# A fused attention and expert kernel: filler products in a tile of their own, the near mask on VectorE, a replanned opening, coarse pairs one inner tile later

## The chip, the cores and the metric

The kernel runs on one core of a Trainium2 chip. The time is the device time of one execution in microseconds (us); three runs of the kernel before gave 1113.57, 1114.93 and 1112.37, median 1113.57. The profile is of one further execution of 1113.12 us, whose span from the first to the last instruction is 1111.3 us; 1.8 us of it lie around the span. Times inside the profile count from the start of the span. Engines: PE is TensorE (PEld its weight loads), DVE is VectorE, ACT is ScalarE, POOL is GpSimd, SP is SyncE, which here only issues transfers.

## The reference

Attention on 8 batches, 8 heads, 576 positions of 64 numbers, the sum of two parts, and behind it a gated feed-forward network over the 8 x 576 = 4608 tokens of 512 numbers:

```python
q_d = q.reshape(B, H, Sd, 4, D).mean(axis=3)          # also k_d, v_d: 144 coarse positions
out_up = np.repeat(sm_attn(q_d, k_d, v_d), 4, axis=2) # every coarse row serves 4 positions
mask = np.abs(pos[:, None] - pos[None, :]) < 4        # band: 7 neighbours
out_local = np.matmul(softmax(where(mask, scale * q @ k.T, -1e9)), v)
x = (out_up + out_local) as (4608, 512)
xn = x / sqrt(mean(x * x) + 1e-6) * rms_g
g = xn @ w_gate                                       # 512 x 1536
out = (g * sigmoid(g) * (xn @ w_val)) @ w_out         # 1536 x 512
```

All is float32.

## The kernel before, in words

**Tiling.** The 4608 tokens are 36 units of 128 tokens; two units make a chunk, so there are 18 chunks of 256 tokens. The feed-forward network of a chunk (class `Forward`) runs over six inner tiles of two 128-wide slices of the 1536: per inner tile 48 products into `ps_h` (L1371: gate and value, each with the high part of the activations against high and low weights and the low part against high weights, so that three products stand for one in float32) and 12 products into `ps_o` (L1409). Before that each chunk needs its activations `xh` and `xl`, turned by eight transposes (L1021) after the mean of squares (L998) and a root by Newton steps (L717 to L719).

**Coarse attention** (class `Coarse`): 32 pairs of heads, four per batch; each is scores (L582), a softmax with its maximum on DVE (L591, L596) and its exponentials on ACT (L601), two transposes (L611), values (L626) and a scaling on DVE (L644), stored to a buffer from which the chunks load it back. **Band attention** (class `Attention`): products with the seven neighbours and sums on DVE (L905, L909, L958, L968) and ACT (L951). Chunk 0 is made otherwise (class `Early`): its band scores run on TensorE. A product of `one_sb` (2^33 times the identity) with `near_sb` (0 on the band, -1 off it) puts the mask into `ps_h` (L1154), the scores are added (L1156), then come the maximum (L1169), the exponentials (L1180), shares, transposes (L1215, L1226), values (L1242), the coarse part (L1249), the copy, squares, root, and the transposes L1287 to `xh` and `xl` (L1290, L1294). `near_sb` is made on POOL by `make_near` from shifted copies of the identity (L1495 to L1501), `one_sb` by `make_one` (L1482).

**Weights** come as raw 64-bit numbers and are decoded in 20 pieces: ACT scales (L315), POOL makes the last bits (L325), DVE joins (L332), ACT rounds the high part (L339), DVE subtracts for the low part (L344, L346).

**What sets the order.** Chunks 0 to 2, band attention up to chunk 3, the first twelve coarse pairs and all decoding are written out by a planner (class `Plan`). Each task has an engine, a cost, a due time, what it follows, and the buffers it takes; `lag` is the time that the plan gives a transfer until it has landed. `RANK`, a table of one number per task, replaces the due times; among the tasks that could start soon on an engine, the lowest number goes first. The order in which the planner takes tasks is the order on each engine's queue, and an engine works its queue strictly in that order. The plan also counts how long TensorE would sit idle before a product (`plan.idle`: from the later of the engine being free and the output's buffer being free), and `heat` (L487 to L500, products at L497) fills 95% of that with filler products of zeros, 256 or 512 columns wide, into the very tile that the next real product will write. Fillers serve nothing but to keep TensorE running; they are a fixed number in the built program, whatever the real times are. From chunk 3 on a loop at the end of the kernel emits the chunk's inner tiles with the next chunk's band attention and two coarse pairs between them, at positions `at` counted in inner tiles; a scheduler settles the rest.

Of the kernel before, what the change touches and what calls it, by code (L numbers as in the profile page):

```python
# [19 lines left out]
P = 128  # L20
# [51 lines left out]
    2040, 2137, 1910, 1295, 1259, 1019, 310, 1083, 1192, 1302, 1748, 1186, 2074, 728, 581, 1321, 2278, 1403,
    1366, 1300, 478, 1512, 1140, 1422, 2046, 1341, 1818, 1238, 667, 1951, 2712, 705, 499, 1901, 2018, 1979,
    2204, 1663, 2103, 1559, 1364, 2075, 916, 2006, 1578, 1699, 2278, 1694, 2367, 1296, 945, 2057, 2643, 1490,
    1510, 1335, 647, 1488, 1579, 1553, 2177, 1304, 2400, 1216, 928, 1667, 2795, 1528, 623, 865, 1035, 1063,
    1094, 1140, 1175, 1800, 2532, 2260, 2066, 2133, 2082, 1659, 1303, 1722, 1285, 1871, 902, 1492, 1229, 1879,
    2256, 2114, 2247, 2458, 2052, 2710, 2316, 2168, 1624, 1870, 1180, 1676, 1980, 1947, 1114, 1296, 1153, 1252,
    1358, 1558, 1420, 2740, 3465, 3179, 2589, 2603, 2821, 3045, 2860, 3141, 2745, 3064, 1135, 2258, 2194, 2453,
    3436, 2937, 2304, 3002, 2299, 3135, 2188, 2846, 1869, 2301, 2073, 1141, 1769, 577, 481, 1035, 729, 1100,
    751, 1131, 1136, 862, 885, 880, 924, 1042, 1067, 1104, 1123, 1252, 1261, 1252, 1268, 1359, 1372, 1266, 1360,  # L80
    1420, 570, 2150, 3901, 229, 1873, 1297, 1427, 1613, 1616, 1493, 1251, 535, 535, 1692, 1181, 1845, 362, 555,
    1526, 1542, 1495, 628, 574, 1558, 1613, 1547, 870, 550, 1724, 1603, 1541, 603, 601, 1502, 1658, 1498, 694,
    803, 1717, 1787, 1623, 730, 803, 1703, 1639, 1759, 603, 734, 1750, 1834, 2679, -522, 1819, 2241, -707, 1556,
    2495, 1719, 1870, 1310, 1386, 526, 1897, 1097, 1237, 467, 1554, 1284, 1521, 1570, 1801, 1383, 1964, 2071,
    1442, 1062, 1458, 1178, 1526, 1413, 1545, 1354, 1672, 1477, 1972, 1505, 2000, 1646, 2226, 1714, 2927, 1604,
    2590, 2691, 2108, 3005, 1733, 1849, 2263, 2127, 2536, 2400, 966, 767, 1687, 2629, 2385, 1032, 962, 1533,
    2769, 2588, 1296, 1000, 1689, 2766, 2444, 972, 1085, 1618, 2709, 2557, 1174, 928, 1756, 2879, 2740, 1197,
    1227, 1795, 2940, 2486, 1020, 1328, 2029, 2881, 2625, 1211, 901, 1799, 3211, 2699, 1944, 2860, 2599, 2325,
    2363, 1854, 2569, 2085, 2452, 3285, 2105, 1880, 2515, 3410, 2111, 189, 468, 382, 275, 215, 340, 149, 612,
    398, 344, 331, 413, 78, 139, 223, -16, 297, 299, 123, 654, 206, 284, 379, 448, 339, 199, 372, 323, 372, 495,  # L90
    274, 501, 349, 374, 476, 297, 205, 639, 350, 599, 622, 633, 614, 767, 500, 501, 474, 392, 520, 627, 410,
    484, 625, 622, 738, 480, 476, 633, 631, 518, 580, 808, 579, 541, 574, 753, 639, 859, 633, 684, 355, 683,
    626, 881, 824, 574, 665, 579, 804, 789, 796, 575, 724, 899, 984, 1209, 799, 1007, 975, 999, 1035, 1216, 611,
    1024, 1136, 957, 342, 679, 455, 477, 1239, 948, 809, 917, 668, 748, 982, 1319, 253, 641, 541, 427, 941,
    1155, 248, 580, 450, 396, 1134, 1143, 769, 692, 810, 848, 716, 821, 633, 703, 871, 950, 1009, 771, 614, 817,
# [1539 lines left out]
```

## Time and profile before

| what | value |
| --- | --- |
| median of three runs | 1113.57 us |
| profiled execution, its span | 1113.12 us, 1111.3 us |
| PE busy | 1077.7 us, 97% |
| DVE, ACT, POOL busy | 924.4 (83%), 603.9 (54%), 194.5 us (18%) |
| L1371 products | 5184 |
| L1409 products | 1296 |
| first L1371 of chunk 0, of chunk 1, of chunk 3 | 88.69, 153.82, 274.31 us |
| granted clock of PE, mean | 0.982 |

How to read it: a row of the timeline or of a group gives a start, a duration, the engine, the line, the operation and the operands as out<-in, with a count behind "x"; what stands in square brackets is the idle time before it and what ended it. In rows of windows the pairs are busy microseconds and instruction counts of each engine. A float32 product counts as two matrix instructions where its operands are not of the rounded kind. PE's durations overlap, since products are pipelined; the distance between starts is the better measure.

### The profile page before, as it was taken

What the parts mean: (1) busy time and instruction counts of PE and PEld (TensorE: products, weight loads), DVE (VectorE), ACT (ScalarE), POOL (GpSimd) and SP (SyncE); (2) the same over time, 40 slices, a digit from 0 to 9 for tenths busy, and PEclk for the clock granted to TensorE, in tenths of its full rate; (3) what the DMA queues carried; (4) which work ended last, traced back from release to release, by engine and by line L of the source; (5) the groups of instructions that cost most, each with busy time, mean ns of one, the idle gap of its engine ahead of it and who ended that gap; (6) DMA issues with size and microseconds to landing.
All of it is one profiled execution on the core that took longest, in us unless ns stands there. A gap on an engine that the chain in (4) does not pass through costs nothing.

```text
span 1111.3 us, 21801 instructions
## 1 busy us (share of the span) xinstructions
PE 1077.7 (97%) x8013; PEld 982.0 (88%) x8013; DVE 924.4 (83%) x1554; ACT 603.9 (54%) x2068; POOL 194.5 (18%) x236
## 2 busy tenths in 40 slices
PE   5899899998999999999999999999999999999997
PEld 4668889897998999999999999999999999999997
DVE  6989988779989898988889898979797988986321
ACT  3865847473747373737474747373737273746111
POOL 8756645231210101010101001100000000000000
PEclk9689989999999999999999999999999999999999
DMA  9787536442663526161525243533131322210000
GB/s 324 261 270 196 132 92 140 96 104 83 136 145 79 131 77 148 50 153 53 138 70 134 64 129 82 130 74 101 39 106 44 96 70 78 72 50 19 1 21 19
DMA packets 79281, 116.84 MB, mean 105 GB/s; under 512 B 32015, under 2 KB 39351, under 8 KB 79173
## 3 DMA queue, kind: packets, MB, share of 16 engines
q1 hardware_dynamic: 47380, 90.50, 26.3%
q0 software_dynamic: 12128, 20.27, 11.5%
q10 hardware_dynamic: 19664, 4.66, 1.9%
q8 instruction: 63, 1.03, 0.4%
q14 instruction: 46, 0.37, 0.1%
HBM read 103.58 MB, written 11.80 MB: 104 GB/s over the span
## 4 chain that ended last, share of the span: by engine, by line
PE 75%; DVE 1%; POOL 0%; issue 0%; ACT 0%; DMA 0%; SPq 0%; DVEq 0%
PE ps_h L1371 45%; PE ps_o L1409 23%; PE ps_a L626 2%; PE ps_a L582 2%; PE ps_a L1021 1%; PE ps_a L611 1%; DVE prod L905 0%; PE ps_a L497 0%; POOL newton L721 0%; DMA q_t<-in_q_band_dram 0%; PE ps_a L998 0%; DVE sc L909 0%; SPq L894 0%; DVE x_t L1008 0%; DVE x_t L968 0%
## 5 line engine op out<-in xcount | busy, mean ns | idle before, releaser
L1371 PE MATMUL ps_h<-xh,w 128*128 128x256 f32 x3456 | 631.2, 280 | 1.4 <-ACT xh L1025 0.7
L1371 PEld LDWEIGHTS ps_h<-xh,w 128*128 128x128 f32 x3456 | 537.3, 188 | 11.1 <-issue 2.3
L1371 PE MATMUL ps_h<-xl,w 128*128 128x256 f32 x1728 | 482.6, 280 | 0.0
L1409 PE MATMUL ps_o<-wo,hs 128*128 128x512 f32 x1296 | 331.8, 399 | 1.8 <-POOL hs L1395 1.0
L1371 PEld LDWEIGHTS ps_h<-xl,w 128*128 128x128 f32 x1728 | 325.3, 188 | 6.5 <-issue 1.9
L951 ACT ACTIVATE prod<-kv,sc 128x64 f32<-128x64 f32 x1088 | 279.8, 407 | 29.5 <-DVE sc L942 20.4
L1409 PEld LDWEIGHTS ps_o<-wo,hs 128*128 128x128 f32 x1296 | 234.6, 190 | 48.1 <-issue 1.7
L968 DVE TENSOR_REDUCE x_t<-prod 128x128 f32<-128x896 f32 x136 | 143.2, 1078 | 42.6 <-PE ps_a L1021 36.7
L1378 ACT ACTIVATE sil<-ps_h 128x512 f32<-128x512 f32 x108 | 64.5, 597 | 159.3 <-PE ps_h L1371 146.8
L905 DVE TENSOR_TENSOR prod<-q_t,kv 128x896 f32<-128x896 f32 x136 | 148.2, 1094 | 1.1 <-DMA q_t<-in_q_band_dram 0.6
L1392 ACT ACTIVATE hs<-sil 128x512 fp32r<-128x512 f32 x108 | 68.1, 630 | 146.9 <-DVE sil L1386 137.8
L909 DVE TENSOR_REDUCE sc<-prod 128x14 f32<-128x896 f32 x136 | 145.1, 1076 | 0.5
L1381 DVE SCALAR_TENSOR_TENSOR sil<-sil,ps_h 128x512 f32<-128x512 f32 x108 | 73.7, 682 | 46.3 <-ACT sil L1378 45.9
L958 DVE TENSOR_TENSOR prod<-sc,kv 128x384 f32<-128x384 f32 (+1 forms) x136 | 110.8, 860 | 0.2
L417 POOL DMA_DIRECT2D qk<-in_qk_sum_dram x42 | 39.3, 963 | 372.1 <-DMA qk<-in_qk_sum_dram 324.3
L1386 DVE SCALAR_TENSOR_TENSOR sil<-sil,ps_h 128x512 f32<-128x512 f32 x108 | 74.4, 689 | 31.6 <-PE ps_h L1371 31.5
L1395 DVE TENSOR_TENSOR hs<-sil,hs 128x512 fp32r<-128x512 f32 x96 | 68.3, 711 | 18.0 <-ACT hs L1392 17.9
L991 ACT ACTIVATE up_t<-x_t 128x128 f32<-128x128 f32 x136 | 41.9, 308 | 47.7 <-DVE x_t L981 29.9
L601 ACT ACTIVATE a_g<-ps_a,m_g 72x144 f32<-72x144 f32 x128 | 46.4, 369 | 22.8 <-DVE m_g L596 21.0
L417 POOL DMA_DIRECT2D vs<-in_v_sum_dram x42 | 38.4, 914 | 82.2 <-DMA vs<-in_v_sum_dram 48.5
L582 PE MATMUL ps_a<-qk 64*72 64x144 f32 x256 | 32.4, 317 | 13.7 <-DVE qk L473 11.9
L691 ACT COPY a_g<-ps_a 72x288 f32<-72x288 f32 x57 | 20.9, 400 | 44.3 <-PE ps_a L611 44.1
(136 smaller groups left out, 851.9 us busy)
## 6 DMA issues: line engine op xcount, KB each, us to landing
kv<-in_k_pad_dram SPq DMA_DIRECT2D x60, 320.0 KB
kv<-in_v_pad_dram SPq DMA_DIRECT2D x60, 320.0 KB
qk<-in_qk_sum_dram POOLq DMA_DIRECT2D x42, 288.0 KB, 4.7
out_dram<-o_sb SPq DMA_DIRECT2D x96, 72.0 KB
vs<-in_v_sum_dram POOLq DMA_DIRECT2D x42, 144.0 KB, 4.1
q_t<-in_q_band_dram SPq DMA_DIRECT2D x150, 36.0 KB
w<-in_w_gate_dram SPq DMA_DIRECT2D x8, 512.0 KB
w<-in_w_val_dram SPq DMA_DIRECT2D x8, 512.0 KB
```

The source lines that it names most:

```text
L417: nc.gpsimd.dma_start(out=t, in_=(qk_sum, v_sum)[i][self.b, j, :, self.half], accum_op=ALU.add)
L905: nc.vector.tensor_tensor(out=pr, in0=bcast(q[:, s0:s0 + 2], 2, NO), in1=window(k, s0), op=ALU.mult)
L909: nc.vector.tensor_reduce(out=self.sc[:, j, par, s0:s0 + 2], in_=self.pr[i], axis=AX.X, op=ALU.add,)
L951: nc.scalar.activation(out=self.pr[i][:, o, s], in_=self.v[j, par][:, s0 + s + o], func=AF.Copy, scale=p[:, s, o:o + 1],)
L958: (nc.vector if engine == "DVE" else nc.gpsimd).tensor_tensor(out=self.pr[i][:, a:b], in0=bcast(p[:, :, a:b].rearrange("p s o -> p o s"), ...
L968: nc.vector.tensor_reduce(out=self.x[j][:, s0:s0 + 2, par], in_=pr.rearrange("p o s d -> p s d o"), axis=AX.X, op=ALU.add,)
L1371: nc.tensor.matmul(out=p[n][:, i], lhsT=wi[:, k], rhs=xi[:, k], start=(m == 0), stop=(m == 3 * KT - 1),)
L1381: nc.vector.scalar_tensor_tensor(out=self.sil[n], in0=self.sil[n], scalar=1.0, in1=self.g[n], op0=ALU.add, op1=ALU.mult,)
L1386: nc.vector.scalar_tensor_tensor(out=self.sil[n], in0=self.sil[n], scalar=0.5, in1=self.v[n], op0=ALU.mult, op1=ALU.mult,)
L1392: nc.scalar.activation(out=self.hs[n][:, 0], in_=self.sil[n], func=AF.Copy)
L1395: (nc.gpsimd if engine == "POOL" else nc.vector).tensor_tensor(out=self.hs[n][:, 1], in0=self.sil[n], in1=self.hs[n][:, 0], op=ALU.subtract,)
L1409: nc.tensor.matmul(out=self.o[j], lhsT=lhs[:, cols], rhs=rhs, start=(f == 0 and m == 0), stop=(f == NF - 1 and m == 2),)
```

## The change

Four edits and a new table.

1. **Filler products.** Until the second unit of chunk 0 makes its values, the fillers go into a tile of their own, one of the two `ps_o` tiles, 512 columns wide, and their number comes from a second count, `plan.gap`, which runs from the moment TensorE is free, so that the wait for an output buffer counts too. After that they are as they were.
2. **Near mask.** `make_near` runs on VectorE, without its second memset and with copies of only the first one to three columns in place of whole copies; it no longer follows `make_one` in the plan. The tasks of `make_one` and `make_side` may start at 3.2 instead of 4.5.
3. **Transfer times.** The plan's `lag` is 4.8 instead of 3.0 for the queries loaded by POOL, 4.8 instead of 2.5 for the coarse rows loaded back, 5.2 instead of 3.0 for the edges, 6.5 instead of 3.0 for the small constants. The first scores follow `one_got`. All 898 numbers of `RANK` are new, and set the due time itself.
4. **Coarse pairs.** In the loop from chunk 3 on, a pair of heads starts at inner tile 1.2 and 3.7 instead of 0.2 and 2.7.

```diff
 RANK = [
-    -191, 26, -38, -38, -158, 58, -11, 182, -9, 532, 96, -192, -174, 137, 126, 652, 291, 633, -15, 139, 540,
+    -37, 56, 29, 38, 46, 24, 113, 129, 137, 55, 64, 68, 135, 142, 150, 165, 170, 176, 181, 159, 191, 215, 227,
...
-            by = RANK[len(self.tasks)] / 10 - options[0][2]
-            options = [(e, c, d + by) for e, c, d in options]
+            first = options[0][2]
+            options = [(e, c, RANK[len(self.tasks)] / 10 + (d - first)) for e, c, d in options]
...
-            self.idle = s - max(known, WARM_AT) if e == "PE" else 0.0
+            self.idle, self.gap = (s - max(known, WARM_AT), s - max(free[e], WARM_AT)) if e == "PE" else (0.0, 0.0)
...
+    spare = {"open": True}
+
     def heat(out, fresh=True):
 
-        n, plan.idle = plan.idle * WARM_SHARE, 0.0
+        n = plan.idle
+        if spare["open"] and made:
+            if "tile" not in spare:
+                spare["tile"] = ps_o.tile([P, DM], FP32, name="ps_o")
+            out, fresh, n = spare["tile"], True, plan.gap
+        n, plan.idle, plan.gap = n * WARM_SHARE, 0.0, 0.0
...
-                         allocs=k_bufs[jp][1:], lag=3.0, sw=len(runs(u))),
+                         allocs=k_bufs[jp][1:], lag=4.8, sw=len(runs(u))),
...
         def value(self, u):
+            if self.y_tag == "ps_o" and (self.y or "tile" not in spare):
+                if "tile" in spare:
+                    heat(spare["tile"])
+                spare["open"] = False
...
-        nc.gpsimd.memset(t, 0.0)
-        nc.gpsimd.memset(u, 0.0)
-        nc.gpsimd.tensor_copy(out=t[:, 1:1 + P], in_=ident_sb)
+        nc.vector.memset(t, 0.0)
+        nc.vector.tensor_copy(out=t[:, 1:1 + P], in_=ident_sb)
         for step, a, b in ((1, t, u), (2, u, t), (3, t, u)):
-            nc.gpsimd.tensor_copy(out=b, in_=a)
-            nc.gpsimd.tensor_tensor(out=b[:, step:], in0=a[:, step:], in1=a[:, :n - step], op=ALU.add)
-        nc.gpsimd.tensor_scalar(out=near_sb, in0=u, scalar1=1.0, scalar2=-1.0, op0=ALU.min, op1=ALU.add)
+            nc.vector.tensor_copy(out=b[:, :step], in_=a[:, :step])
+            nc.vector.tensor_tensor(out=b[:, step:], in0=a[:, step:], in1=a[:, :n - step], op=ALU.add)
+        nc.vector.tensor_scalar(out=near_sb, in0=u, scalar1=1.0, scalar2=-1.0, op0=ALU.min, op1=ALU.add)
...
-    one_got = task("POOL", 0.6, make_one, -70, not_before=4.5)
-    one_side.append(task("DVE", 0.25, make_side, -60, not_before=4.5))
+    one_got = task("POOL", 0.6, make_one, -70, not_before=3.2)
+    one_side.append(task("DVE", 0.25, make_side, -160, not_before=3.2))
     near_got += [
-        task("POOL", 5.6, make_near, -60, [one_got], allocs=[buf("sil"), buf("sil")]),
+        task("DVE", 1.9, make_near, -160, allocs=[buf("sil"), buf("sil")], not_before=3.4),
...
-                at = 0.2 + 5.0 * i / n
+                at = 1.2 + 2.5 * i
```

The changed program has its line numbers some 7 to 11 higher behind the first edits: its L504, L589, L618, L633 are L497, L582, L611, L626 of before, L901, L905 to L912, L1005, L1028 are L894, L898 to L905, L998, L1021, L1161 and L1163 are L1154 and L1156, L1420 is L1409.

**POOL at the start.** Behind the constants that every program sets, the rows of before (the edges of chunk 0's values are `kv`, the queries of chunk 1 `q_t`):

```order
L1135 DMA kv<-in_v_pad_dram 32x1x64 x4
L1506 COPY wo_1_107<-ident_sb 72x256
...
L894 DMA q_t<-in_q_band_dram 24x1x256
L1482 ISA
L1482 TENSOR_SCALAR one_sb<-ident_sb 128x128
L1495 MEMSET sil 128x140
...
L1501 TENSOR_SCALAR near_sb<-sil 128x140
L325 TENSOR_SCALAR w_2_130<-w_2_130 128x1024 x2
```

and of the change:

```order
L1516 COPY wo_1_118<-ident_sb 72x256
L1142 DMA kv<-in_v_pad_dram 32x1x64 x4
L1493 ISA
L1493 TENSOR_SCALAR one_sb<-ident_sb 128x128
L901 DMA q_t<-in_q_band_dram 32x1x256
...
L1146 TENSOR_TENSOR kv<-kv,side_sb 64x512 x2
L481 TENSOR_TENSOR vs<-w_0_134 72x512 x2
L481 TENSOR_TENSOR vs<-vs,w_0_134 72x512 x2
```

One block of four query transfers now stands ahead of `one_sb` instead of two, the mask is gone from this queue, and the placing of the edges and one more addition of `vs` have come to it.

**TensorE at its start.** Before:

```order
L582 MATMUL ps_a<-qk 72x144 x4
L497 LDWEIGHTS one_sb
L497 MATMUL ps_a<-zero_sb,one_sb 72x256
...
L611 MATMUL ps_a<-ident_sb,a_g 72x72 x4
L582 MATMUL ps_a<-qk 72x144 x4
```

Now:

```order
L504 LDWEIGHTS one_sb
L504 MATMUL ps_o<-zero_sb,one_sb 128x512
...
L1161 MATMUL ps_h<-near_sb,one_sb 128x272
L1163 MATMUL ps_h<-w_1_102,hs 128x136 x2
...
L589 MATMUL ps_a<-qk 72x144 x4
```

The first coarse scores, which led the queue, now stand behind seven fillers and two masked band scores of chunk 0.

**TensorE between the mean of squares of chunk 1 and chunk 1's transposes.** Before:

```order
L582 MATMUL ps_a<-qk 72x144 x4
L998 MATMUL ps_a<-ss,same_sb 128x8
L497 LDWEIGHTS one_sb
L497 MATMUL ps_o<-zero_sb,one_sb 128x512
...
L611 MATMUL ps_a<-ident_sb,a_g 72x72 x4
...
L626 MATMUL ps_a<-vs,a_g 72x64 x8
L1021 MATMUL ps_a<-ident_sb,x_t 128x128 x8
```

Now:

```order
L589 MATMUL ps_a<-qk 72x144 x4
L1005 MATMUL ps_a<-ss,same_sb 128x8
L1420 MATMUL ps_o<-wo_2_1295,hs 128x512
...
L618 MATMUL ps_a<-ident_sb,a_g 72x72 x8
...
L1028 MATMUL ps_a<-ident_sb,x_t 128x128 x4
L633 MATMUL ps_a<-vs,a_g 72x64 x8
L1028 MATMUL ps_a<-ident_sb,x_t 128x128 x4
```

Nine fillers that stood behind the mean are gone, and 18 products of L1420 stand between the mean and the first transpose where 18 of L1409, the nine fillers and the coarse values stood.

In all, the queue of TensorE up to the first feed-forward product holds 176 fillers of 512 columns and 9 of 256 (before: 79 and 107), and behind it 3 and 18 (before: 9 and 38).

More of the change, by code (lines that the diff above doesn't have):

```diff
@@ L852, in plan @@
             for j in range(2):
-                load = task("ACT", 1.3 if len(spans(2 * c + j)) == 1 else 2.6, lambda j=j: self.load_up(j), T - 30, up_ready, allocs=[ups[j]], lag=2.5, hw=2 * len(spans(2 * c + j)))
+                load = task("ACT", 1.3 if len(spans(2 * c + j)) == 1 else 2.6, lambda j=j: self.load_up(j), T - 30, up_ready, allocs=[ups[j]], lag=4.8, hw=2 * len(spans(2 * c + j)))
                 add = task(
@@ L1046, in plan @@
                 ve = buf("kv")
-                e_got = task("POOL", 1.6, lambda u=u: self.load_edges(u), -60, allocs=[ve], lag=3.0, sw=2)
+                e_got = task("POOL", 1.6, lambda u=u: self.load_edges(u), -60, allocs=[ve], lag=5.2, sw=2)
                 v_got = task("SP", 0.4, lambda u=u: self.load_values(u), -90 + 12 * u, dma=0.26 * MB, hw=1)
@@ L1057, in plan @@
                         "PE", 0.8, lambda u=u, n=n: self.score(u, n), at - TAIL,
-                        [sums[0, n // 2].q_got, near_got[0], *(used["qk"][-1:] if n % 2 else [])],
+                        [sums[0, n // 2].q_got, near_got[0], one_got, *(used["qk"][-1:] if n % 2 else [])],
                         allocs=sps[n:n + 2] if n % 2 == 0 else [], uses=[sps[n], sums[0, n // 2].q_buf],
@@ L1518, in load_small @@
         nc.gpsimd.dma_start(out=same_sb, in_=same_tok)
-    small = task("POOL", 4.0, load_small, -40, not_before=2.5, lag=3.0, sw=6)
-    one_got = task("POOL", 0.6, make_one, -70, not_before=4.5)
-    one_side.append(task("DVE", 0.25, make_side, -60, not_before=4.5))
+    small = task("POOL", 4.0, load_small, -40, not_before=2.5, lag=6.5, sw=6)
+    one_got = task("POOL", 0.6, make_one, -70, not_before=3.2)
+    one_side.append(task("DVE", 0.25, make_side, -160, not_before=3.2))
     near_got += [
-        task("POOL", 5.6, make_near, -60, [one_got], allocs=[buf("sil"), buf("sil")]),
+        task("DVE", 1.9, make_near, -160, allocs=[buf("sil"), buf("sil")], not_before=3.4),
         task("POOL", 0.6, make_spread, -50, not_before=2.5),
```

92 rows, old and new, of the table RANK are left out of this document.

## The prediction

> **What bounds the kernel now.** I read the page's shares first, then four stretches cut at the first feed-forward product of chunk 0 (88.7), of chunk 1 (153.8) and of chunk 3 (274.3), then TensorE's waits, then the start row by row.
>
> ```profile
> PE 1077.7 (97%) x8013; PEld 982.0 (88%) x8013; DVE 924.4 (83%) x1554; ACT 603.9 (54%) x2068; POOL 194.5 (18%) x236
> ```
>
> ```profile
> 0.00:88.70 88.70, 70.64 (x421) 49.60 (x421) 72.81 (x115) 55.49 (x121) 61.31 (x71) 0.85 0.83 274
> 88.70:153.80 65.10, 60.56 (x428) 52.95 (x426) 60.05 (x90) 39.17 (x118) 37.99 (x46) 0.95 0.54 140
> 153.80:274.30 120.50, 115.40 (x882) 105.25 (x880) 102.09 (x174) 65.67 (x242) 45.66 (x63) 0.99 0.48 110
> 274.30:1111.30 837.00, 831.10 (x6287) 774.22 (x6287) 689.48 (x1178) 443.61 (x1590) 49.56 (x57) 1.00 0.34 84
> ```
>
> The columns behind the stretch are its length, then PE, PEld, DVE, ACT, POOL busy, the granted clock of PE, the DMA share and GB/s. The last 837.0 us are TensorE's alone: 831.1 busy at full clock. The time to be won lies before 274.3. There the first 88.7 us hold no feed-forward work, and much of TensorE's "busy" is filler:
>
> ```profile
> 0.00:88.70 88.70, 33.95 (x186) 21.17 (x186) 0.85 0.83 274
> 88.70:153.80 65.10, 5.27 (x18) 2.15 (x16) 0.95 0.54 140
> ```
>
> These are the fillers alone (PE and PEld busy). Real products took 70.64 - 33.95 = 36.7 us of the first stretch. The rest of it is waiting:
>
> ```profile
> PE ps_a L582 <- DVE qk L473: 11.9, 1, 11.9
> PE ps_a L998 <- ACT up_t L991: 4.4, 2, 2.9
> PE ps_a L1021 <- DVE x_t L1008: 2.1, 1, 2.1
> PE ps_h L1154 <- ACT w L1180: 1.9, 2, 1.3
> PE ps_a L582 <- DVE xl L644: 1.7, 1, 1.7
> PE ps_a L1215 <- ACT prod L691: 1.4, 1, 1.4
> PE ps_o L1409 <- POOL hs L1395: 1.0, 1, 1.0
> PE ps_a L1215 <- DVE xl L644: 0.9, 1, 0.9
> PE ps_o L1409 <- DVE hs L1395: 0.8, 1, 0.8
> PE ps_h L1371 <- ACT xh L1025: 0.7, 1, 0.7
> ```
>
> Before 88.7 TensorE waits 11.9 for its first work and 1.9 + 1.7 + 1.4 + 0.9 = 5.9 inside; behind 88.7 the rows give 4.4 + 2.1 + 1.0 + 0.8 + 0.7 = 9.0; asked of the time past 300 alone, the view of waits is empty. And the clock is halved for two stretches of the opening:
>
> ```profile
> 26.60:33.50 6.90, 6.90 (x44) 5.86 (x45) 6.52 (x13) 4.65 (x14) 4.08 (x4) 0.51 0.94 267
> 43.70:64.20 20.50, 15.23 (x64) 11.24 (x65) 17.85 (x28) 14.22 (x38) 15.16 (x13) 0.50 0.84 295
> ```
>
> That is 27.4 us at half clock.
>
> **Start and mask.** What stands ahead of TensorE's first products:
>
> ```profile
> 1.38 2.41 POOL L1135 DMA_DIRECT2D kv<-in_v_pad_dram  x4 [0.93 <-POOLq L1623]
> 4.09 2.21 POOL L894 DMA_DIRECT2D q_t<-in_q_band_dram  x4
> 9.79 0.90 POOL L1482 TENSOR_SCALAR one_sb<-ident_sb 128x128 bf16<-128x128 f32 x1
> 13.36 1.24 POOL L1500 TENSOR_TENSOR sil<-sil 128x138 f32<-128x138 f32 x1
> 16.06 0.41 POOL L1500 TENSOR_TENSOR sil<-sil 128x137 f32<-128x137 f32 x1
> 16.56 1.08 POOL L1501 TENSOR_SCALAR near_sb<-sil 128x140 bf16<-128x140 f32 x1
> 6.49 1.06 ACT L467 COPY hs<-w 128x512 f32<-128x512 f32 x1 [3.76 <-DMA w<-in_qk_sum_dram]
> 2.99 0.21 DVE L1487 TENSOR_REDUCE side_sb<-ident_sb 64x8 f32<-64x64 f32 x1 [2.10 <-DMA ident_sb<-in_ident_dram]
> 7.92 0.68 DVE L1139 TENSOR_TENSOR kv<-kv,side_sb 64x512 f32<-64x512 f32 x1 [4.72 <-DMA kv<-in_v_pad_dram]
> ```
>
> On POOL one block of four query transfers leaves the place ahead of `one_sb`; the block of edges, a copy and one query block end at 4.09 + 2.21 = 6.3, so `one_sb` is there at 6.3 + 0.9 = 7.2 instead of 10.7. The mask's ten instructions cost between 10 x 0.21 = 2.1 (L1487) and 10 x 0.68 = 6.8 (L1139, 512 columns); with 140 columns they are nearer the first: 2.1, from 3.2 to 5.3. It hides in DVE's wait: VectorE did nothing between 3.2 and 7.92, and the first operand lands at 6.49. With that cover gone it would cost 2.1 on DVE. Before, `near_sb` was ready at 16.56 + 1.08 = 17.6; now the band scores can run from 6.49 + 1.06 = 7.55, filling what was the 11.9 wait.
>
> **The opening up to the first feed-forward product.** TensorE's prices:
>
> ```profile
> 21.61 0.28 PE L1154 MATMUL ps_h<-near_sb,one_sb 128*128 128x272 bf16 x1
> 22.94 0.29 PE L1154 MATMUL ps_h<-near_sb,one_sb 128*128 128x272 bf16 x1
> 74.82 7.96 PE L497 MATMUL ps_a<-zero_sb,one_sb 128*128 128x512 bf16 x36
> 285.13 2.36 PE L497 MATMUL ps_a<-zero_sb,one_sb 128*72 128x256 bf16 x20
> ```
>
> A filler of 512 columns takes 7.96/36 = 0.221, one of 256 2.36/20 = 0.118. The 176 + 9 fillers now ahead of L1371 are 38.9 + 1.1 = 40.0 us at full clock (before: 34.0 busy). A masked score is 22.94 - 21.61 = 1.33 us, where the plan has 0.8; its fillers were counted with the short price, so the 8 x 0.53 = 4.2 us come on top and no gap takes them up. Real work is 36.7 if as slow as before, some 33 if the clock holds (an estimate: of 22.1 busy us in the two halved stretches most was real work, and the scores did not slow down in them). Waits inside: 0 to 5.9. TensorE's own sum is 7.2 + 40.0 + 33 = 80.2 at least and 7.2 + 40.0 + 36.7 + 5.9 = 89.8 at most. VectorE's: up to the second L1294 the queue has as many rows more (the mask, two L905, one L909, one copy) as fewer (two L1139, one L481, two L332, one L346), so 72.8 us from 6.5 on give 79.3; with all of the 88.7 - 72.8 - 7.9 = 8.0 us that it idled inside, 87.3. Both bounds say 80 to 90. I take 84.5, the middle: **4.2 us won** of 88.7.
>
> The Trainium skill, TensorE: Matmul & The Clock Gate, What's actually happening, halves the clock after an idle window of about 3.4 us. The rows disagree in part: 26.60 to 33.50 ran at 0.51 with TensorE busy for all 6.90 us. By that rule the fillers keep the clock whole and the sum is 80.2; by the row, stretches of small products may still be halved, which is why I do not take 80.2.
>
> **Chunk 0 to chunk 1.**
>
> ```profile
> 88.38 0.68 DVE L1294 TENSOR_TENSOR xl<-ps_a,xh 128x512 fp32r<-128x512 f32 x1
> 140.30 4.00 PE L497 MATMUL ps_o<-zero_sb,one_sb 128*128 128x512 bf16 x9
> 143.74 2.83 PE L1409 MATMUL ps_o<-wo,hs 128*128 128x512 f32 x6
> 145.65 0.66 DVE L1008 TENSOR_TENSOR x_t<-x_t,rinv 128x512 f32<-128x512 f32 x1
> 148.22 0.68 DVE L1008 TENSOR_TENSOR x_t<-x_t,rinv 128x512 f32<-128x512 f32 x1
> 150.82 1.04 PE L1021 MATMUL ps_a<-ident_sb,x_t 128*128 128x128 f32 x8
> ```
>
> Nine fillers held TensorE from 140.30 to 143.74 although L1409 behind them waited for nothing, and the transposes came at 150.82 when their inputs were there at 146.3 and 148.9. The change drops the nine (3.4 us) and puts the first transpose ahead of the coarse values, so it can start when the first half is normed. From 88.7 to 153.8 VectorE was busy 60.05 of 65.10, so what TensorE gains ahead of the mean it waits for: I leave that wait (the larger of L998's two, 2.9) as it is, and take 65.1 - 4.1 = 61.0. Bounds: 60.05, VectorE without a gap; 66, if 3 to 4 us of wait take the fillers' place and a halved window follows.
>
> **Chunk 1 to chunk 3.** TensorE's busy 115.4 of 120.5 is the floor; the waits there are 5.1. The order changes in every part and no row prices it, so half of it: 118.0, range 115.4 to 125 (as many new waits again). One coarse pair more falls before the cut and one fewer behind it, which adds nothing.
>
> **Chunk 3 to the end.** Fillers fall from 31 to 7 of 256 columns: 24 x 0.118 = 2.8, nothing waiting for what they covered. The coarse pairs' shift moves instructions on engines that wait for nothing on TensorE's path; zero, since no wait of TensorE lies past 300; cover gone would mean a few L1021 waits like the 2.1 above. 837.0 - 2.8 = 834.2, range 832 to 838.
>
> **The sum.** 84.5 + 61.0 + 118.0 + 834.2 = 1097.7 span; the profiled execution, 1113.12, is 1.8 longer than its span and 0.45 below the median of 1113.57: 1097.7 + 1.8 + 0.4 = **1100**.
>
> **Rivals.**
> - *VectorE eats it.* VectorE is busy 72.81 + 60.05 of the first 153.8, decoding and chunk 1's band; if its idle 21 us do not shrink, chunk 1 starts near 153 whenever chunk 0 did. For it: the waits on L991 and L1008. Against: 7.9 of the 21 are the start, which the change fills. 153 + 118.0 + 834.2 + 2.2 = 1107.
> - *POOL is held up.* The same addition took 0.41 at 16.06 and 1.24 at 13.36, beside VectorE's additions. POOL now has two L1139 and a fourth L481 ahead of the first coarse values; three of them ahead of VectorE's own L481, each 0.8 longer or more, make some 3 us of wait in two queues: 1103. The Trainium skill, SBUF — State Buffer, Who interferes with whom, says that a VectorE instruction with two SBUF inputs and a reading GpSimd instruction shut each other out for a whole instruction; the two rows fit it.
> - *It does not do what it says.* The new transfer times are as far off as the old ones, the opening ends at 88 and new waits match the old: 1113.6 less the 2.8 of late fillers, about 1111 to 1113.
> - *Slower: the clock stays halved.* The fillers are a fixed load on TensorE, and at half clock each costs 0.221 more. If the opening has as much halved time as before, 27.4 us or eight windows of 3.4, and the queue is now nearly all filler and product without a gap, each window costs its 1.7 us: 80.2 + 5.9 + 13.7 = 99.8 for chunk 0, and 99.8 + 61 + 118 + 834.2 + 2.2 = 1115. From seven windows on it is slower. For it: the halving at 26.60 without idleness. Against: the second, longer halving fell where TensorE was busy only 15.23 of 20.50, and fillers now stand in such gaps.
>
> **How the numbers follow.** Forecast 0.52, own range 1093 to 1106; VectorE 0.18; POOL 0.10; nothing 0.08; slower 0.12. The measurement of this kernel can tell 0.2%, 2.2 us, from no change. Faster: 0.52 + 0.18 + 0.10 = 0.80; same 0.08; slower 0.12. For eight in ten the range must take VectorE's case and part of "nothing": 1090 to 1112; the low end is the sum of all lower bounds, 80 + 60 + 115.4 + 832 + 2.2 = 1089.6.
>
> **What would show it.** First L1371 near 84.5, and the clock above 0.9 before it; band scores ahead of 12 us; no fillers of 4 us behind L998, the next chunk's L1371 some 61 us after the first; chunk 3 near 263; from there 834. Wrong if TensorE's first stretch has the forecast's fillers but halved windows, if L998 waits over 6 us, or if waits appear past 300.

## The result, and the profile after

The change made the kernel slower. Five runs gave 1118.39 to 1126.07 us, median 1120.39; five of the kernel before 1109.84 to 1114.93, median 1113.57. The ratio is 1.0065, 95% interval 1.0040 to 1.0089: 0.65% or 7 us, where 1100 was forecast. The profiled execution is the longest of the five, 1126.07 us with a span of 1124.3; the experiments below give four more profiles of the same opening. Line numbers after the change are 7 to 11 higher: L1382 is the first products (L1371), L1420 the second (L1409), L1028 the transposes (L1021), L1015 the norm (L1008), L504 the fillers (L497), L912 and L916 the band scores (L905, L909), L724 to L726 the Newton steps on VectorE and L728 to L731 those on POOL.

The windows view of the change, cut like the forecast's: first L1382 of chunks 0, 1 and 3 (columns as there).

```profile
0.00:92.05 92.05, 80.46 (x419) 45.08 (x420) 76.80 (x123) 54.10 (x119) 61.54 (x65) 0.93 0.77 264
92.05:154.69 62.64, 58.08 (x427) 52.25 (x425) 59.07 (x89) 40.30 (x118) 39.59 (x49) 0.97 0.59 146
154.69:287.64 132.95, 120.46 (x918) 109.41 (x916) 105.52 (x190) 72.16 (x268) 41.55 (x61) 0.97 0.47 109
287.64:1124.30 836.66, 829.89 (x6227) 771.18 (x6227) 684.94 (x1164) 439.21 (x1564) 46.60 (x54) 0.99 0.33 82
```

Before stood 88.70, 65.10, 120.50 and 837.00. The third row carries the loss: 12.45 us more, of which TensorE was busy for only 5.1. Part of that busy time is work that moved: one coarse pair more now stands between the first products of chunks 1 and 3, and one fewer behind it (an estimate from TensorE's rows in the run with both roots back below: scores 0.71, transposes 0.67, values 1.22, some 2.6 us). TensorE's waits, from the waits view of the first 330 us:

```profile
PE ps_o L504 <- POOL one_sb L1493: 7.5, 1, 7.5
PE ps_a L1028 <- DVE x_t L1015: 7.4, 2, 5.8
PE ps_a L618 <- ACT a_g L608: 4.1, 3, 1.8
PE ps_a L1005 <- ACT up_t L998: 2.7, 1, 2.7
```

The start is as forecast (7.5 in place of 11.9). New is the wait of the transposes for the norm at chunk 2, 5.8 us; at chunk 3 it is 1.6 us, where 2.1 stood before. The chain of waits, asked of 205 to 290 us (start, length, what), says what stands behind the first:

```profile
207.45 5.44 DMA qk<-in_qk_sum_dram
213.31 4.10 DMA qk<-in_qk_sum_dram
217.78 0.88 POOL qk L417
220.91 1.74 DVE x_t L1015
222.69 1.11 PE ps_a L1028 x4
```

and the timeline of POOL shows how a transfer comes to hold up a norm:

```profile
213.31 0.87 POOL L417 DMA_DIRECT2D qk<-in_qk_sum_dram  x1 [4.94 <-DMA qk<-in_qk_sum_dram]
213.88 0.53 POOL L728 TENSOR_TENSOR newton<-rinv 128x8 f32<-128x8 f32 x1
...
217.78 0.88 POOL L417 DMA_DIRECT2D qk<-in_qk_sum_dram  x1 [2.51 <-DMA qk<-in_qk_sum_dram]
218.39 0.50 POOL L728 TENSOR_TENSOR newton<-rinv 128x8 f32<-128x8 f32 x1
...
220.67 0.20 POOL L731 TENSOR_TENSOR rinv<-rinv,newton 128x8 f32<-128x8 f32 x1
```

Before, chunk 2's root ran on VectorE, and from the mean to its last step took 2.4 us (VectorE's timeline, before):

```profile
206.38 0.17 DVE L706 TENSOR_SCALAR rms<-ps_a 128x8 f32<-128x8 f32 x1 [1.23 <-PE ps_a L998]
...
208.60 0.17 DVE L719 SCALAR_TENSOR_TENSOR rinv<-newton,rinv 128x8 f32<-128x8 f32 x1
```

The new table puts it on POOL, where it took 11.6 us. There it stands in the queue between loads that add to a tile (L417), each of which waits until the load before it has landed. VectorE had the mean at 209.27,

```profile
209.27 0.17 DVE L713 TENSOR_SCALAR rms<-ps_a 128x8 f32<-128x8 f32 x1 [0.84 <-PE ps_a L1005]
```

and the root's first Newton step ran at 213.88 and the second round's at 218.39, each right behind such a load. POOL stood idle for 4.94 and 2.51 us before the two loads, with the root behind them in its queue. The Trainium skill, DMA: Bandwidth & Descriptors, Rules for kernel authors, asks for just that wait between an accumulating transfer and any other access of the same bytes; the two rows show it.

Chunk 3's root went the other way, from POOL to VectorE. VectorE's timeline there (three preparing instructions and nine Newton steps, of which the ones left out lie between):

```profile
271.37 0.15 DVE L713 TENSOR_SCALAR rms<-ps_a 128x8 f32<-128x8 f32 x1
271.44 1.07 DVE L916 TENSOR_REDUCE sc<-prod 128x14 f32<-128x896 f32 x1
...
274.03 0.15 DVE L716 TENSOR_SCALAR rinv<-rms 128x8 uint32<-128x8 uint32 x1
274.10 1.08 DVE L912 TENSOR_TENSOR prod<-q_t,kv 128x896 f32<-128x896 f32 x1
275.10 0.16 DVE L717 TENSOR_SCALAR rinv<-rinv 128x8 uint32<-128x8 uint32 x1
...
277.13 0.15 DVE L724 SCALAR_TENSOR_TENSOR newton<-rinv 128x8 f32<-128x8 f32 x1
...
280.29 0.15 DVE L726 SCALAR_TENSOR_TENSOR rinv<-newton,rinv 128x8 f32<-128x8 f32 x1
280.66 1.28 DVE L1015 TENSOR_TENSOR x_t<-x_t,rinv 128x512 f32<-128x512 f32 x2
```

Some 1.9 us of small instructions take 9.1 us, with band scores of 1.07 us and gates of 0.68 between them. That alone is no loss against before: there the three preparing instructions stood in VectorE's queue as well, and the root took 12.0 us to its last step on POOL:

```profile
254.87 0.15 DVE L706 TENSOR_SCALAR rms<-ps_a 128x8 f32<-128x8 f32 x1
```

```profile
266.67 0.20 POOL L724 TENSOR_TENSOR rinv<-rinv,newton 128x8 f32<-128x8 f32 x1
```

What is longer than before at chunk 3 is the recorded half clock, 10.2 us where 3.4 stood (from 269.0). The two stretches of half clock at the roots, in the windows view of the change:

```profile
220.40:227.20 6.80, 4.51 (x15) 3.82 (x16) 4.25 (x6) 3.53 (x13) 3.28 (x5) 0.50 0.14 26
285.20:295.50 10.30, 8.43 (x48) 7.69 (x49) 9.73 (x18) 10.30 (x46) 1.57 (x2) 0.50 0.60 145
```

### The profile page after: what moved, and what is told of

The parts are those of the page before. It is cut to its first block, busy times and chain, and to the rows that moved or that the text cites. A ratio compares the mean times of both kernels' runs of the same rounds, so it can differ in the third digit from the quotient of the medians.

```text
span 1124.3 us, 21773 instructions
## 1 busy us (share of the span) xinstructions
PE 1088.9 (97%) x7986; PEld 977.9 (87%) x7986; DVE 926.3 (82%) x1563; ACT 605.8 (54%) x2067; POOL 189.3 (17%) x227
## 4 chain that ended last, share of the span: by engine, by line
PE 78%; DMA 9%; DVE 6%; ACT 2%; issue 2%; POOL 1%; SPq 0%; ACTq 0%; DVEq 0%; POOLq 0%
PE ps_h L1382 47%; PE ps_o L1420 23%; PE ps_a L633 2%; DMA qk<-in_qk_sum_dram 2%; PE ps_a L589 2%; DMA kv<-in_k_pad_dram 2%; DMA w<-in_w_val_dram 2%; PE ps_a L1028 1%; DMA vs<-in_v_sum_dram 1%; PE ps_a L618 1%; DVE x_t L975 1%; ACT prod L958 1%; DMA w<-in_v_pad_dram 1%; DVE prod L912 1%; DVE sc L916 1%
## 5 line engine op out<-in xcount | busy, mean ns | idle before, releaser
L1382 PE MATMUL ps_h<-xh,w 128*128 128x256 f32 x3456 | 638.9, 281 | 2.9 <-DVE sil L1392 2.0
L1382 PEld LDWEIGHTS ps_h<-xh,w 128*128 128x128 f32 x3456 | 540.2, 189 | 14.8 <-issue 4.4
L1382 PE MATMUL ps_h<-xl,w 128*128 128x256 f32 x1728 | 483.6, 280 | 0.0
L1420 PE MATMUL ps_o<-wo,hs 128*128 128x512 f32 x1296 | 331.9, 399 | 0.3 <-POOL hs L1406 0.3
L1382 PEld LDWEIGHTS ps_h<-xl,w 128*128 128x128 f32 x1728 | 326.0, 189 | 5.8 <-issue 1.9
L1420 PEld LDWEIGHTS ps_o<-wo,hs 128*128 128x128 f32 x1296 | 234.4, 190 | 43.3 <-POOL hs L1406 0.8
L912 DVE TENSOR_TENSOR prod<-q_t,kv 128x896 f32<-128x896 f32 x136 | 148.0, 1093 | 0.7
L916 DVE TENSOR_REDUCE sc<-prod 128x14 f32<-128x896 f32 x136 | 146.0, 1075 | 0.4
L965 DVE TENSOR_TENSOR prod<-sc,kv 128x384 f32<-128x384 f32 (+1 forms) x136 | 108.2, 845 | 0.1
L417 POOL DMA_DIRECT2D qk<-in_qk_sum_dram x42 | 38.7, 920 | 413.8 <-DMA qk<-in_qk_sum_dram 319.8
L1406 DVE TENSOR_TENSOR hs<-sil,hs 128x512 fp32r<-128x512 f32 x98 | 66.8, 682 | 17.9 <-ACT hs L1403 17.9
L998 ACT ACTIVATE up_t<-x_t 128x128 f32<-128x128 f32 x136 | 42.0, 309 | 44.9 <-DVE x_t L988 42.2
L417 POOL DMA_DIRECT2D vs<-in_v_sum_dram x42 | 37.2, 885 | 77.3 <-DMA vs<-in_v_sum_dram 70.2
L504 PEld LDWEIGHTS <-one_sb 128*128 128x128 bf16 (+1 forms) x206 | 21.9, 111 | 31.2 <-issue 9.8
L504 PE MATMUL ps_o<-zero_sb,one_sb 128*128 128x512 bf16 x123 | 36.2, 444 | 7.5 <-POOL one_sb L1493 7.5
```

Of the source, the lines that this page charges most:

```text
L417: nc.gpsimd.dma_start(out=t, in_=(qk_sum, v_sum)[i][self.b, j, :, self.half], accum_op=ALU.add)
L912: nc.vector.tensor_tensor(out=pr, in0=bcast(q[:, s0:s0 + 2], 2, NO), in1=window(k, s0), op=ALU.mult)
L916: nc.vector.tensor_reduce(out=self.sc[:, j, par, s0:s0 + 2], in_=self.pr[i], axis=AX.X, op=ALU.add,)
L965: (nc.vector if engine == "DVE" else nc.gpsimd).tensor_tensor(out=self.pr[i][:, a:b], in0=bcast(p[:, :, a:b].rearrange("p s o -> p o s"), ...
L1382: nc.tensor.matmul(out=p[n][:, i], lhsT=wi[:, k], rhs=xi[:, k], start=(m == 0), stop=(m == 3 * KT - 1),)
L1406: (nc.gpsimd if engine == "POOL" else nc.vector).tensor_tensor(out=self.hs[n][:, 1], in0=self.sil[n], in1=self.hs[n][:, 0], op=ALU.subtract,)
```

## The experiments

Each line is one profiled execution, cut at the first product of chunks 0, 1, 2, 3 and 5 (product 1, 289, 577, 865 and 1441 in the timeline), and then the ratio of all its runs to the kernel before, run on the same chip in the same session. One profile can lie 4 to 6 us from its kernel's median (the change 1126.07 of 1120.39; both roots back with old pairs 1106.78 of 1111.37), so stages are compared over several. From chunk 3 on the scheduler may set another order of products in each build, so the last two columns compare builds and not single edits. The coarse pair that moved ahead of chunk 3 counts in the middle columns of every row with the new order.

| kernel | to chunk 0 | 0 to 1 | 1 to 2 | 2 to 3 | 3 to 5 | 5 to end | ratio (95%) |
| --- | --- | --- | --- | --- | --- | --- | --- |
| before | 88.7 | 65.1 | 62.8 | 57.7 | 120.6 | 716.4 | 1 |
| before, again | 89.8 | 67.1 | 67.6 | 56.0 | 120.6 | 716.4 | |
| the change | 92.1 | 62.6 | 74.8 | 58.2 | 118.4 | 718.3 | 1.0065 (1.0040 to 1.0089) |
| chunk 2's root back | 86.9 | 61.9 | 67.1 | 59.0 | 118.6 | 718.7 | 1.0036 (1.0014 to 1.0058) |
| both roots back | 88.8 | 63.9 | 68.1 | 55.3 | 114.8 | 718.3 | 0.9971 (0.9952 to 0.9990) |
| before, roots as in the change | 89.2 | 67.8 | 63.9 | 61.2 | 123.3 | 715.9 | 1.0072 (1.0051 to 1.0092) |
| half the fillers | 86.2 | 65.9 | 72.1 | 57.9 | 117.4 | 718.3 | 1.0045 (1.0026 to 1.0063) |
| no fillers | 89.1 | 63.2 | 72.0 | 58.5 | 117.3 | 718.3 | 1.0055 (1.0035 to 1.0075) |
| VectorE's work added | 94.1 | 62.3 | 74.4 | 58.4 | 118.2 | 718.3 | 1.0106 (1.0083 to 1.0130) |
| old pairs | 88.9 | 63.7 | 72.2 | 58.2 | 118.7 | 717.5 | 1.0065 (1.0040 to 1.0090) |
| before, later pairs | 89.2 | 67.1 | 62.9 | 56.5 | 120.9 | 718.4 | 1.0008 (0.9992 to 1.0024) |
| before, later pairs and own tile | 93.0 | 63.8 | 62.6 | 60.1 | 123.6 | 718.6 | 1.0063 (1.0042 to 1.0085) |
| both roots back, old pairs | 87.0 | 62.9 | 67.5 | 55.1 | 115.0 | 717.5 | 0.9966 (0.9951 to 0.9980) |
| both roots back, old fillers | 90.7 | 60.9 | 68.8 | 55.2 | 115.0 | 718.2 | 0.9967 (0.9955 to 0.9980) |

**Chunk 2's root on VectorE.**

```diff
-            newton(self.r, self.inv, engine)
+            newton(self.r, self.inv, "DVE" if self.c == 2 else engine)
```

> The changed kernel, with chunk 2's root (its three Newton rounds) on VectorE, where the kernel before has it, in place of POOL. Theory A: the loss between chunk 1 and chunk 2 (74.8 us in the profile of the change, 62.8 before) comes from the root standing on POOL behind two accumulating loads that wait for earlier transfers. Then TensorE's 5.8 us wait ahead of chunk 2's transposes goes, the half-clock stretch behind it (6.8 us) with it, chunk 1 to chunk 2 takes 64 to 67 us, and the time is 6 to 9 us under the change, some 1112 to 1114. Rival B: the new order as a whole is late there, and the root only the last to show it; then the wait goes to another releaser, the stretch stays above 72 us and the time within 2 us of the change's 1120.4.

Chunk 1 to 2 took 67.1 us, against 72.0 to 74.8 in the five profiles with that root on POOL; the wait of chunk 2's transposes is gone from the waits view and no half clock stands there. The order of TensorE's products up to chunk 3 is that of the change, so the wait and the stretch hang on this root. But the time fell by only 0.29% of the ratio, some 3 us. Half of A: the place is right, the size is not, and chunk 3's wait of 1.6 us and its 10.2 us of half clock are still there.

**Both roots back.**

```diff
+            newton(self.r, self.inv, {2: "DVE", 3: "POOL"}.get(self.c, engine))
```

> The changed kernel with both roots on the engines where the kernel before has them: chunk 2's on VectorE, chunk 3's on POOL. Theory A: chunk 3's root, which in the change is cut up between VectorE's band products and takes from 271.4 to 280.5 us, is what makes chunk 3's start late and is followed by the 10.2 us of half clock that every profile of the new order shows there; on POOL, whose queue is empty there, it ends earlier, the half clock shrinks to 3.4 us, chunk 2 to chunk 4 takes 3 to 5 us less than the 120.6 of the run with chunk 2's root alone moved, and the time is 2 to 5 us under that run's 1117.8. Rival B: VectorE's band products hold the norm up whatever engine has the root; then chunk 2 to chunk 4 stays within 1.5 us and the time within 2 us of 1117.8.

A has the place and the sign, and the gain is larger than its ranges: chunks 2 to 4 took 113.7 us (55.3 + 58.4) where 120.6 stood, no half clock is left there, and the kernel is now 0.29% faster than before, 1111.60 us (twelve runs, 1109.11 to 1116.21). POOL's and VectorE's timeline at chunk 3:

```profile
266.91 0.20 POOL L728 TENSOR_TENSOR newton<-rinv 128x8 f32<-128x8 f32 x1 [24.30 <-DVE rinv L717]
...
271.26 0.20 POOL L731 TENSOR_TENSOR rinv<-rinv,newton 128x8 f32<-128x8 f32 x1
```

```profile
271.50 1.29 DVE L1015 TENSOR_TENSOR x_t<-x_t,rinv 128x512 f32<-128x512 f32 x2 [1.20 <-POOL rinv L731]
```

POOL's twelve Newton steps take 4.5 us in a queue with nothing else in it, longer than the nine on VectorE in the change (277.13 to 280.44, 3.3 us), and from the mean to its end the root takes 8.5 us against 9.1. So the root itself is hardly shorter. What fell are TensorE's waits around it, with the same order of products up to chunk 3's start: for the norm from 1.6 to 0.6, for a copy of VectorE ahead of the second transposes (L700) from 1.4 to 0.3, and two behind them of 0.9 and 1.0 are gone. How much of that is the norm's place in VectorE's queue and how much the nine queue places that the other work there regained was not separated. No half clock is recorded between 147 and 1106 us. The windows view puts the forecast's last two stretches (cut some 0.2 us behind the first products of chunks 1 and 3) at

```profile
152.90:276.30 123.40, 118.53 (x917) 107.63 (x917) 104.42 (x186) 68.77 (x253) 42.20 (x61) 1.00 0.52 116
276.30:1109.10 832.80, 826.63 (x6227) 767.73 (x6226) 687.29 (x1168) 441.41 (x1579) 46.63 (x54) 1.00 0.34 83
```

**The kernel before, with the two roots as the change has them.**

```diff
+            newton(self.r, self.inv, {2: "POOL", 3: "DVE"}.get(self.c, engine))
```

> The kernel before with the two roots where the change has them: chunk 2's on POOL, chunk 3's on VectorE. Theory A: these two places carry the loss whatever the order; the time rises by 3 to 8 us over the kernel before, with a wait of TensorE ahead of chunk 2's transposes and some 10 us of half clock at chunk 3. Rival B: the harm needs the accumulating loads just ahead of the root on POOL, and in the order before POOL's queue is empty from 205 to 210 us; then chunk 2's root costs 2 us at most, being 3.4 us on POOL against 1.9 on VectorE, and the time is within 3 us.

The time rose by 0.72%, as much as by the whole change. Here both expectations are half right: chunk 2's root met an empty POOL and cost little (chunk 1 to 2 63.9 us, 62.8 and 67.6 in two profiles of before),

```profile
207.48 0.97 POOL L417 DMA_DIRECT2D vs<-in_v_sum_dram  x1
210.22 0.20 POOL L721 TENSOR_TENSOR newton<-rinv 128x8 f32<-128x8 f32 x1 [1.77 <-DVE rinv L710]
...
213.32 0.20 POOL L724 TENSOR_TENSOR rinv<-rinv,newton 128x8 f32<-128x8 f32 x1
```

while chunk 3's was torn apart on VectorE (15.6 us from the mean to its end, the three rounds of Newton steps from 267.54 to 274.26) and the time from chunk 2 to 3 went from 56 or 57.7 to 61.2, with 10.2 us of half clock at 278:

```profile
267.54 0.16 DVE L717 SCALAR_TENSOR_TENSOR newton<-rinv 128x8 f32<-128x8 f32 x1
...
274.26 0.17 DVE L719 SCALAR_TENSOR_TENSOR rinv<-newton,rinv 128x8 f32<-128x8 f32 x1
```

So the two harms are different: on POOL it is the loads ahead, which this run does not have, and on VectorE the queue itself. The second is the weaker proof: in this build four coarse transposes (L611) also moved ahead of chunk 3's first product, where they waited 2.0 us for exponentials beside the 2.7 us for the norm, and no run has the one without the other.

**Half the fillers, and none** (everywhere, the other planned work in the same order).

```diff
-WARM_SHARE = 0.95
+WARM_SHARE = 0.5      # and 0.0
```

> The changed kernel with about half of the filler products everywhere (the share of each gap that is filled is 0.5 in place of 0.95; the order of all other work is unchanged). Theory A: in the opening the fillers themselves are what TensorE's queue is made of (49.6 of its first 92.05 us), and VectorE waits for them too (6.2 us for scores); then chunk 0's first feed-forward product comes at 86 to 89 us in place of 92.1, and the time falls by 3 to 6 us. Rival B: fewer fillers halve the clock for longer stretches and eat it; then the first product comes at 91 us or later, with more than the 13.6 us of recorded half clock ahead of it, and the time is within 2 us of the change.

> The changed kernel without any filler product, the other work in the same order. Theory A (fillers bound the opening): real products and TensorE's waits for VectorE set the start of chunk 0, 85 to 90 us, even at half clock for more of the time. Rival B (the clock decides): most of the first 90 us run at half clock, real products of 33 us become 60 or so, and chunk 0 starts at 92 us or later; the time is 0 to 8 us above the change's.

With 185, 90 and 0 fillers ahead of it, chunk 0 began at 86.9 to 92.1 (five profiles of the change's opening), 86.2 and 89.1 us. Without fillers the opening ran at half speed: sixteen coarse values took 2.1 to 2.2 us each time, where 1.20 to 1.25 stand in the change at full clock, and three of chunk 0's products take 0.64 us from start to start until 95.3 (93.99 to 94.63) and 0.34 from then on (96.02 to 96.36). The clock's record begins at 95.3.

```profile
93.99 0.41 PE L1382 MATMUL ps_h<-xl,w 128*128 128x256 f32 x1
...
96.02 0.28 PE L1382 MATMUL ps_h<-xl,w 128*128 128x256 f32 x1
```

```profile
0.00:89.10 89.10, 52.71 (x235) 37.48 (x235) 74.04 (x121) 54.22 (x119) 62.24 (x63) 1.00 0.80 273
```

TensorE was busy for 52.7 of the 89.1 us, at half speed, and it was enough. Leaving them out cost nothing that these runs can tell (1.0055 beside 1.0065). Both starts came where the two Theories A had them, but with half of them the time fell by some 2 us and not 3 to 6, without them by 1, all inside the noise; neither rival B had the start. So neither fillers nor clock set the start of chunk 0. VectorE is busy 74.0 us in that row.

**VectorE's work added**: the low part of the first six weight pieces subtracted twice.

```diff
+            for _ in range(2 if len(twice) <= 6 else 1):
                 (the subtraction into lo)
```

> The changed kernel, with the subtraction for the low part of the first six weight pieces on VectorE done twice: six further instructions of 1.2 to 1.5 us, some 7.5 us of VectorE's time ahead of chunk 0's root. Theory A: VectorE's queue sets the start of chunk 0, which is why 185, 90 and no fillers gave 87 to 92, 86.3 and 89.1 us; then the start comes 5 to 8 us later than in the runs with the same opening (86.9 to 92.1), at 93 to 99, and the time is 4 to 8 us above the change. Rival B: TensorE's queue or the transfers of the weights set it and VectorE has slack; then the start stays within 2 us of 86.9 to 92.1.

```profile
0.00:94.10 94.10, 79.40 (x420) 43.58 (x420) 83.69 (x127) 54.14 (x119) 59.75 (x63) 0.91 0.79 262
```

VectorE was busy 83.7 us in place of 74.4 to 76.8, chunk 0 began at 94.1, 5.3 us behind the mean of the five profiles (88.7), and the ratio rose by 0.41%, 4.6 us. The start follows VectorE's load and not TensorE's. What VectorE waits for in the rest differs: for band scores, which stand behind fillers, 6.2 us in the change, 2.0 to 3.5 in the four others with the same opening and 0.2 without fillers, where it waited for POOL instead (3.4 us for additions, 2.2 for last bits). Which of these waits could be won stays open.

**The pairs and the fillers' tile, singly.** The change with the pairs at their old places:

```diff
-                at = 1.2 + 2.5 * i
+                at = 0.2 + 5.0 * i / n
```

> The changed kernel with the coarse pairs of the last loop at inner tiles 0.2 and 2.7 again, as before. The forecast priced the shift at nothing: chunk 3 to the end within 1 us of the change at the same clock, and the time within 2 us of 1120.4. Rival: the later pairs, which let the time from chunk 3 on start with fewer interruptions, save or cost some tenths per chunk; over 13 chunks with pairs 3 us or more.

No difference in time (1.0065 both); 0.8 us less from chunk 5 on. The kernel before with the later pairs, alone and with the fillers' own tile:

> The kernel before with one edit of the change alone: the later coarse pairs. With the fillers' own tile beside it the kernel before lost 7 us (1122.7), the chunks from the sixth on took 57.1 us where they took 56.6, and chunk 3 to the end 842.0 where it took 837. Theory A: all of that behind chunk 3 is the shift's; then chunk 3 to the end again takes 840 to 843, the chunks 57.0 to 57.1, and the time is 3 to 5 us above the kernel before, 1118 to 1121. Rival B: it is the fillers' own tile that cost (chunk 0 at 93.1); then the shift alone is within 2 us of the kernel before.

> The kernel before, with its own table, transfer times and mask, and only two edits of the change: the fillers' own tile and the later coarse pairs. Theory A: the loss of the change is in the new order, and the two edits are worth nothing or a little: 1110 to 1116, within 3 us of the kernel before, whose 56.6 us per chunk with coarse pairs stay within 0.15. Rival B: the fillers in a tile of their own (a fixed load) or the shift cost by themselves: the first product of chunk 0 over 92 us, or 56.9 to 57.0 per chunk, and 1117 or more.

Alone, the pairs cost 2.0 us from chunk 5 on (57.1 us per chunk in place of 56.6) and in the time nothing that can be told (1.0008). With the own tile the kernel before loses 0.63%. Its fillers are a load there (TensorE's timeline ahead of chunk 0):

```profile
74.57 13.10 PE L504 MATMUL ps_a<-zero_sb,one_sb 128*128 128x512 bf16 x49
87.51 0.60 PE L1298 MATMUL ps_a<-ident_sb,x_t 128*128 128x128 f32 x4
87.94 2.98 PE L504 MATMUL ps_a<-zero_sb,one_sb 128*128 128x512 bf16 x13
90.75 0.60 PE L1298 MATMUL ps_a<-ident_sb,x_t 128*128 128x128 f32 x4
91.19 2.11 PE L504 MATMUL ps_h<-zero_sb,one_sb 128*128 128x512 bf16 x9
```

71 fillers around the transposes, part of them at half clock: chunk 0 at 93.0. The same profile also has 10.2 us of half clock at chunk 3 with the root on POOL. There, twelve coarse transposes (L618) stand ahead of chunk 3's first product and wait for exponentials and a copy (waits view from 219 to 300 us), while with the pairs alone they stand behind it and no half clock is recorded there:

```profile
PE ps_a L618 <- ACT a_g L608: 1.9, 2, 1.7
PE ps_a L618 <- DVE a_g L700: 0.7, 1, 0.7
```

So a root on VectorE is not the only thing that brings a long halving at that place. In the change's order the two edits make no difference once the roots are back:

> The change with both roots moved back (1111.6) and the coarse pairs at their old places. If the shift costs here what it cost in the kernel before, some 0.4 us per chunk, the chunks fall to 56.6 and the time to 1107 to 1109; if it costs only the 0.1 us per chunk that the change itself showed between the two (57.0 and 56.9), the time stays within 2 us of 1111.6.

> The change with both roots moved back (1111.6) and the fillers as before, in the tile of the next product and counted by the old rule. Theory A: VectorE sets the start of chunk 0 and the fillers do not matter; 86 to 90 us and within 2 us of 1111.6. Rival B: the fillers' own tile adds a load on TensorE's queue that the old rule does not; then the start comes 2 us or more under the 86.9 to 92.1 of the same order with the own tile, and the time is 2 to 4 us shorter.

0.9966 and 0.9967 beside 0.9971; the medians are 1111.37, 1110.99 and 1111.60 us. All three beat both kernels; between them the runs do not choose.

**The kernel before, once more.**

> The kernel before, unchanged, for a second profile of its stages. If its opening varies from run to run as that of the change does (86.9 to 92.1 us in three profiles of the same opening), the start of chunk 0 differs from 88.7 by up to 3 us; if it does not vary, it comes at 88 to 89.5. Chunk 1 to chunk 2 and the chunks from the fifth on should repeat: 62.8 and 56.6 us within 0.5.

The start of chunk 0 repeats within 1.1 us and the late chunks exactly; chunk 1 to 2 does not, 67.6 in place of 62.8. TensorE waited 2.9 us for the mean there (1.5 in the first profile), 3.4 us of half clock stand behind it, and VectorE waited for coarse rows loaded back:

```profile
DVE x_t L981 <- DMA up_t<-up: 4.4, 2, 3.0
```

The forecast was made on a profile with less of it:

```profile
DVE x_t L981 <- DMA up_t<-up: 2.3, 1, 2.3
```

## Why the prediction was wrong, step by step

- **Chunk 1 to chunk 3 (118.0, range to 125): the failed step.** "The order changes in every part and no row prices it, so half of it." The stretch took 132.95, and the means of the profiles with the change's roots are 73.1 (five) and 58.4 (six), 131.5: 13.5 of the 20 us between forecast and result. Put both roots back and it is 122.6 to 124.0 (three profiles), with no half clock in it. The change of engine of two roots could be read from the order of POOL and VectorE beforehand; the step halved the waits instead of asking for each product's last input where it now stands and what is queued ahead of it. Bound "as many new waits again" was too small: chunk 2's late norm cost its wait of 5.8 us and had a half-clocked stretch behind it, and both went with the root. Some 2.6 us of what is left with both roots back is the coarse pair that "adds nothing": it adds nothing to the sum, but it belonged in this term and out of the last one.
- **The opening (84.5): wrong by its size.** The start came as said, `one_sb` at 7.5, and the mask hid on VectorE (3.3 to 5.2). But the middle between the two sums took VectorE's idle time to be half won. VectorE was busy 74.4 to 76.8 us in the five profiles (72.8 forecast; two more band scores and the mask are in it) and idle for another 12.0 to 15.3: 88.7 in the mean, as before (88.7 to 89.8 in four profiles of that opening). TensorE's sum was no bound: its fillers cost 49.6 us, not 40.0 (the windows view of the fillers alone, the change),

```profile
0.00:92.05 92.05, 49.58 (x185) 19.78 (x185) 0.93 0.77 264
```

  and leaving all of them out changed nothing.
- **Chunk 0 to 1 (61.0): right in sign, 2 us short.** 61.9 to 63.9 in five profiles, 63.0 in the mean, inside the bounds; 65.1 to 67.8 in four with the old order. That the nine fillers did it is not shown: the kernel before with the fillers' own tile keeps all nine and took 63.8 too.
- **Chunk 3 to the end (834.2): near, in part by luck.** In the change 836.7; with both roots back 833.1. There the stretch to chunk 5 is 5.8 us shorter than before, 2.8 by the fillers as forecast and the rest about what the moved coarse pair costs, and the "zero" of the shifted pairs was 2.0 in the old order and 0.8 in the new. In the change, chunk 3's late start reaches into it as well (3 to 5: 118.4, against 114.8).
- **The rivals.** "VectorE eats it" has the bound of the opening right, but not that chunk 1 starts near 153 whenever chunk 0 did: in the five profiles it began at 148.8 to 154.7, and earlier when chunk 0 did. "POOL is held up" named the right engine and the wrong place. "Slower: the clock stays halved" had the sign, by a mechanism that the run without fillers rules out: the opening at half clock to its end began chunk 0 at 89.1.

The loss adds up from the means: against the kernel before (89.2, 66.8, 64.4, 56.7, 120.7, 716.4; two to four profiles each), the change has 88.7, 63.0, 73.1, 58.4, 118.5 and 718.4, together 5.9 us more; 6.8 was measured. Moving the two roots alone is worth 0.94% of the ratio (1.0065 to 0.9971), more than the whole loss. But only chunk 2's place is a loss against before. From chunk 2 to 5 the change takes 176.9 us where 177.4 stood, fillers and a coarse pair fewer; with chunk 3's root on POOL it takes 170.1 to 170.2. There VectorE's place eats a gain of the new order.

## What to carry to other kernels

When a planner's table is replaced, follow each short serial step that TensorE's next product hangs on (here a root) through the new order: which engine it landed on, and what stands ahead of it in that queue. An instruction of 0.2 us behind a load that waits for another load's landing costs what the landing costs (here 4.94 and 2.51 us). In a queue shared with long work look at TensorE's waits and not at the chain's own length: two places of one root differed by 0.6 us in length and, with the other work of that queue, by some 4 us in TensorE's waits. And before crediting a filled gap on one engine, take that engine's work away altogether and see whether the end of the stage moves.

## What the hardware showed unexpectedly

- TensorE starts at half speed, and the granted clock does not show it: the row of 10 to 20 us reads 1.00, while thirteen fillers took 0.39 us each (0.221 at full clock). In this profile the clock's record begins at 19.0 us, in the run without fillers at 95.3.

```profile
10.00:20.00 10.00, 10.00 (x35) 5.09 (x34) 6.06 (x10) 2.58 (x9) 6.04 (x4) 1.00 1.05 288
```

```profile
14.60 5.12 PE L504 MATMUL ps_o<-zero_sb,one_sb 128*128 128x512 bf16 x13
```

- The same opening had its half-clock stretches elsewhere in each profile: from 39.4 and 66.7 us in the change (13.6 us in all), 29.2, 39.4 and 56.5 with chunk 2's root back (10.2), 64.8 with both (6.8). The Trainium skill, TensorE: Matmul & The Clock Gate, What's actually happening, has the clock start low and rise after a busy window that does not begin with the kernel, so that its phase differs from run to run; the three profiles fit that, but do not show the cause. It has about 3.4 us of sustained activity raise the clock, and in the run without fillers 52.7 busy us of the first 89.1 did not, 6.9 us on end without a wait among them (7.86 to 14.79).
